# Token rows of a two-stage MLP kernel: stored two tiles at a time, fetched whole, and laid out through DRAM

## The chip, the cores and the metric

The kernel runs on one core of one Trainium2 chip. The metric is the time on the device in microseconds (us); lower is better. A core has a matrix engine (TensorE, PE here, with its weight loads as PEld), VectorE (DVE), ScalarE (ACT), GpSimd (POOL), SyncE (SP), and 16 DMA engines that move data between DRAM and the on-chip memory. SP only issues DMAs in this kernel; POOL issues the indirect ones, whose rows an index picks.

## The reference

Three steps follow one another. All inputs are fp32.

```python
# 1 retention attention: 8 batches x 8 heads, 576 x 64 each, no softmax
scores = (q @ k.T) / 8
ret = scores * where(rel >= 0, gamma[h] ** rel, 0)
x = (ret @ v)                      # as rows: [4608 tokens, 512]
# 2 top-1 mixture of 8 experts, 512 -> 1024 -> 512
idx = argmax(x @ w_gate); gate_w = softmax(x @ w_gate)[idx]
x = gate_w * (maximum(x @ w1[idx], 0) @ w2[idx])
# 3 MLP 512 -> 2048 -> 512
r = maximum(x @ w_in, 0); out = (r * r) @ w_out
```

## The kernel before, in words

Matrix products are made from two or three passes: an fp32 number is split into a high and a low part, and high times high, high times low and low times high are added. The last stage also saves products by a Strassen-like scheme. The program is written out by hand in the order in which it stands on each engine (`manual_schedule`), so each engine runs its instructions in the order of the code.

**Attention** handles 36 tiles of 128 tokens, one per pass of a loop over t. SP loads the tile of four passes ahead (`load(t + 4)`, L364, `in<-att`, up to 1 MB). PE makes the scores (L387), DVE masks them (r, L393), PE makes the output (L435, L439) and the running state (L411), DVE scales it (x, L447) and turns 32 x 32 blocks of it (xr, L449, in one of three buffers). A tile's `put` runs in the next pass: four DMAs of 64 KB (L456, `x_d<-xr`) that write the tile's rows to x_d in DRAM, with the columns of a row permuted in blocks of 32. Small matmuls (lg) give the gate's logits, which go to l_d in DRAM. From these, each token gets a place at its expert: an expert has CT = 5 tiles of 128 places, of which `gidx` names the token to fetch and `sidx` the row to write. The first two tiles of expert 0 are fetched early (lead, L270).

**Experts** run as 64 units, u = 8e + f: expert e and one eighth f of its 1024 hidden columns. A unit is `first` (L806 to L808: 24 matmuls of 320 columns, the hidden values), then ACT and DVE split these (hh L812, hl L813), then `second` (L830 to L832: 15 matmuls of 512 columns, accumulated over the eight units). Units 0 to 5 do a part of the work ahead and are shorter. Beside a unit stand:

- SP loads the weights of seven units ahead (raw, L107) into one of two buffers; ACT and DVE split them one unit later (L113, L115). Side jobs prepare the last stage's weights: SP loads craw (L129), DVE and ACT split it, SP stores it in ws_d (L183, L211).
- POOL fetches the next expert's rows into xs, the only buffer of its kind: for tile i at f = i one `gather`, that is a `tick` (L1050, a 1x1 addition that reads this unit's hidden values and so waits for them) and four indirect DMAs (L270), one for each quarter of a row, since the quarters have to land in four groups of 32 partitions. At f = 5 it fetches five tiles of logits (glg), at f = 7 `finish` scatters the expert's five result tiles to y_d (L291).
- `transp(e+1, i)` at f = i + 2 turns 32 x 32 blocks of xs (DVE, L778) and splits the result into high and low (ACT L782, DVE L783): the columns that the next expert's `first` reads. Because of the permuted columns in x_d, that DVE transpose is all it takes. Expert 0's tiles are fetched whole and turned on PE.

The indices of the quarters, qidx = 4 gidx + a, are made once by `spread`: four matmuls with a table `sel` (256 KB, loaded at L651) and one DVE operation (L788, L789).

**The last stage** reads y_d, and its PE work runs without a pause to the end of the program.

Of the kernel before, what the change touches and what calls it, by code (L numbers as in the profile page):

```python
# [20 lines left out]
NE = 8  # L21
CAP = 640
CT = CAP // 128
NS = NE * CT
# [3 lines left out]
LEAD = 2  # L28
MORE = 6
TINY = 2.0 ** -15 * 1.125  # L30
GROUPS = [(0, 8), (8, 16), (16, 24), (24, 30), (30, 36)]
# [18 lines left out]
def body(ctx, tc, att, tab_v, tab_x, masks, wg, ident, pick, cst, wu, wd, out):  # L50
# [21 lines left out]
    x_d = dram.tile([NTOK, 512], F32, name="x_d")  # L72
    l_d = dram.tile([NTOK, NE], F32, name="l_d")
    y_d = dram.tile([NTOK, 512], F32, name="y_d")
# [4 lines left out]
    sel = places.tile([128, 4, 128], F32, name="sel")  # L79
    ones = places.tile([128, 128], BF16, name="ones")  # L80
# [11 lines left out]
    over = places.tile([1, 1], I32, name="over")  # L92
    gidf = places.tile([128, NS], F32, name="gidf")
    qidx = places.tile([128, 4, NS], I32, name="qidx")

# [160 lines left out]

    def indices(rt, n, inv, gi, si, gf=None):
# [4 lines left out]
        for o in (gi, gf):  # L262
            if o is not None:
                vec.tensor_scalar(out=o, in0=f, scalar1=-1.0, scalar2=0.0, op0=ALU.add, op1=ALU.max)
        g = rt.tile([128, n], F32, tag="g", name="g")
        vec.tensor_scalar(out=g, in0=inv[:, 0:n], scalar1=0.0, scalar2=FAR, op0=ALU.is_equal, op1=ALU.mult)
        vec.scalar_tensor_tensor(out=si, in0=f, scalar=-1.0, in1=g, op0=ALU.add, op1=ALU.add)

    def fetch_rows(xs, src, index):
        pool.indirect_dma_start(  # L270
            out=xs, out_offset=None, in_=src, in_offset=bass.IndirectOffsetOnAxis(ap=index, axis=0),
        )

    def fetch_logits(sm, index, n):
        lg = sm.tile([128, n, NE], F32, tag="lg", name="glg")
        for i in range(n):
            fetch_rows(lg[:, i], l_d[:, :], index[:, i:i + 1])
        return lg


    x_q = x_d.rearrange("n (a c) -> (n a) c", a=4)

# [44 lines left out]
    rt_ps = scope(chain, "rt_ps", 1, PSUM, side="right")  # L327
    with ExitStack() as es:
        tabs = scope(es, "tabs", 1)
# [4 lines left out]
        xr_p = scope(es, "xr_p", 3)  # L334
        sc_ps = scope(es, "sc_ps", 3, PSUM)
# [10 lines left out]

        in_t, vs_t, r_t, st_acc, xp_t = {}, {}, {}, {}, {}
        lead_s = []
# [71 lines left out]
        def out_x(t):  # L420
# [215 lines left out]
        for t in range(NT):  # L636
# [60 lines left out]
    def columns():  # L697
        return [xt_p.tile([128, 4, CAP], F32R, tag=f"xt{s}", name=f"xt{s}") for s in range(2)]
# [52 lines left out]
    with ExitStack() as es:  # L751
# [3 lines left out]
        acc_a = scope(es, "acc_a", 1, PSUM, reuse="tile")  # L755
        xs_t, xt_t, lg_t, h_t, acc, gate = {}, {}, {}, {}, {}, {}

        def gather(e, tiles):
            if e not in xs_t:
                xt_t[e] = columns()  # L760
                xs_t[e] = xs_p.tile([128, CT, 4, 128], F32, tag="xs", name="xs")
            for i in tiles:
                j = CT * e + i
                if e == 0:
                    fetch_rows(xs_t[e][:, i].rearrange("p q c -> p (q c)"), x_d[:, :], gidx[:, j:j + 1])
                    continue
                for q in range(4):
                    fetch_rows(xs_t[e][:, i, q], x_q, qidx[:, q, j:j + 1])

        def transp(e, i):  # L770
# [12 lines left out]
            return lambda: vec.tensor_tensor(out=lo, in0=src, in1=hi.bitcast(F32), op=ALU.subtract)  # L783

        def spread():
            ps = l1_ps.tile([128, 4, NS], F32, tag="l1", name="qi")
            for q in range(4):
                pe.matmul(ps[:, q], sel[:, q], gidf, start=True, stop=True)  # L788
            vec.tensor_scalar(  # L789
                out=qidx, in0=ps, scalar1=4.0, scalar2=cf[:, C_A:C_A + 1], op0=ALU.mult, op1=ALU.add  # L790
            )

# [157 lines left out]
        steps[4]()  # L950
        indices(rt, NS, inv, gidx, sidx, gidf)
        gather(0, range(LEAD, CT))
# [19 lines left out]
        y_p = scope(es, "y_p", 5, reuse="tile")  # L972
        sm = scope(es, "sm", 2, reuse="tile")
        lp = scope(es, "lp", 1, reuse="tile")
        pools["stg"] = scope(early, "stg", 2, side="right", reuse="tile")
# [30 lines left out]
        second(5, tiles)  # L1006
        lg_t[0] = fetch_logits(sm, gidx[:, 0:CT], CT)
        first(0, (1,))
        spread()

        for u in range(NU):
# [32 lines left out]
            if v >= NU + 2:  # L1044
                stream(w_d, v - NU - 2)
            if e + 1 < NE:
                if f <= CT:
                    tick = sm.tile([1, 1], F32, tag="tick", name="tick")
                    here = h_t[u][0][0:1, 0:1].bitcast(F32)
                    pool.tensor_tensor(out=tick, in0=here, in1=here, op=ALU.add)  # L1050
# [4 lines left out]
            if e + 1 < NE:  # L1055
                turns = {3: [0], 4: [1], 5: [2], 6: [3, 4]} if e == 0 else {i + 2: [i] for i in range(CT)}
                rests += [transp(e + 1, i) for i in turns.get(f, [])]
            for f_ in rests[:1]:
# [426 lines left out]
```

## Time and profile before

| what | us |
|---|---|
| median of three runs | 1406.72 |
| the three runs | 1402.28, 1406.72, 1415.77 |
| profiled execution, its time | 1416.54 |
| profiled execution, its span | 1414.7 |

The profiled execution has 1.8 us outside its span, and is the longest of the four. The span divides into attention (to about 198 us, with expert 0's first steps at its end), the experts (to about 640 us), and the last stage. The rows are shown further down; shares of busy time over the whole span average over these three.

### The profile page before, as it was taken

To read this page: it belongs to the slowest core of one execution; us is meant where nothing else is said; L and a number is where in the kernel's file an instruction comes from. 1 tells how busy PE (TensorE), PEld (TensorE's weight loads), DVE (VectorE), ACT (ScalarE), POOL (GpSimd) and SP (SyncE) were. 2 spreads that over 40 slices of the span, in tenths; PEclk is the share of its full clock that TensorE was granted. 3 is DMA by queue.
4 is the path that set the end of the run, shared out by engine and by line. 5 is a ranking of instruction groups with operands and counts; after the bars stand their busy time and mean duration, and the time that the engine had idled before them with its cause. 6 is when DMAs were issued, how large, how long until landed. Compare 5 with 4: busy or idle time off the path is not lost.

```text
span 1414.7 us, 21636 instructions
## 1 busy us (share of the span) xinstructions
PE 1359.7 (96%) x8121; PEld 1161.9 (82%) x8121; DVE 831.8 (59%) x1512; ACT 547.0 (39%) x1064; POOL 375.4 (27%) x408
## 2 busy tenths in 40 slices
PE   8988898999989999899999999999999999999998
PEld 6877787888878889798988888888888888888887
DVE  5666765686967768673785466245742556334422
ACT  1222233453434445342554444244432444234321
POOL 2223345747456474611231013000210003000000
PEclk9999999999999999999999999999999999999999
DMA  9999844666666675656776666567666666665563
GB/s 318 291 287 290 249 137 153 219 217 210 210 197 193 199 246 186 208 173 251 275 272 224 212 233 225 205 208 229 222 234 212 214 207 230 212 234 183 204 212 115
DMA packets 107713, 311.03 MB, mean 220 GB/s; under 512 B 20430, under 2 KB 55758, under 8 KB 85584
## 3 DMA queue, kind: packets, MB, share of 16 engines
q1 hardware_dynamic: 97728, 288.41, 59.9%
q0 software_dynamic: 9872, 21.15, 5.1%
q8 instruction: 66, 1.08, 0.3%
q14 instruction: 47, 0.39, 0.1%
HBM read 257.98 MB, written 52.58 MB: 220 GB/s over the span
## 4 chain that ended last, share of the span: by engine, by line
PE 77%; DMA 10%; issue 6%; POOL 2%; DVE 2%; ACT 1%; another core or an unknown queue 1%; SPq 1%; POOLq 0%; DVEq 0%; ACTq 0%
PE b L1149 23%; PE fa L1223 9%; PE fa L1221 9%; PE fa L1222 9%; DMA in<-att 5%; PE l L808 4%; PE acc L830 4%; PE l L807 4%; PE l L806 4%; PE acc L831 4%; PE acc L832 4%; DMA raw<-wu 1%; POOL xs L270 1%; DMA x_d<-xr 1%
## 5 line engine op out<-in xcount | busy, mean ns | idle before, releaser
L1149 PE MATMUL b<-xt,wq 128*128 128x512 f32 (+1 forms) x1296 | 264.7, 362 | 1.8 <-ACT xt L743 0.7
L1149 PEld LDWEIGHTS b<-xt,wq 128*128 128x128 f32 x1296 | 220.9, 188 | 40.6 <-ACT xt L743 1.1
L1221 PE MATMUL fa<-wq,ch 128*128 128x512 f32 x576 | 224.3, 389 | 0.0
L1223 PE MATMUL fa<-wq,cl 128*128 128x512 f32 x576 | 224.3, 389 | 0.0
L1222 PE MATMUL fa<-wq,ch 128*128 128x512 f32 x576 | 224.3, 389 | 0.0
L1211 DVE TENSOR_TENSOR cl<-g,ch 128x512 fp32r<-128x512 f32 (+1 forms) x160 | 108.9, 689 | 173.7 <-ACT ch L1210 171.2
L734 POOL TENSOR_TENSOR xsum<-yf 128x256 f32<-128x256 f32 x80 | 64.1, 809 | 452.3 <-DVE yf L722 386.9
L270 POOL DMA_INDIRECT xs<-x_d,qidx x140 | 154.9, 1106 | 40.0 <-issue 34.9
L1210 ACT ACTIVATE ch<-g 128x512 fp32r<-128x512 f32 (+1 forms) x160 | 91.5, 584 | 182.4 <-PE fa L1222 181.4
L806 PE MATMUL l<-xt,w 128*128 128x320 f32 (+1 forms) x480 | 150.5, 314 | 6.7 <-issue 5.0
L808 PE MATMUL l<-xt,w 128*128 128x320 f32 (+1 forms) x480 | 150.6, 314 | 5.1 <-issue 5.0
L807 PE MATMUL l<-xt,w 128*128 128x320 f32 (+1 forms) x480 | 150.7, 314 | 4.3 <-issue 4.2
L831 PE MATMUL acc<-w,hh 128*128 128x512 f32 x320 | 128.5, 402 | 3.0 <-issue 3.0
L830 PE MATMUL acc<-w,hh 128*128 128x512 f32 x320 | 129.1, 403 | 2.2 <-issue 1.8
L832 PE MATMUL acc<-w,hl 128*128 128x512 f32 x320 | 127.9, 400 | 2.4 <-issue 2.4
L1223 PEld LDWEIGHTS fa<-wq,cl 128*128 128x128 f32 x576 | 108.1, 188 | 22.5 <-DVE cl L1211 0.2
L1222 PEld LDWEIGHTS fa<-wq,ch 128*128 128x128 f32 x576 | 108.2, 188 | 22.5
L1221 PEld LDWEIGHTS fa<-wq,ch 128*128 128x128 f32 x576 | 108.1, 188 | 22.3
L812 ACT ACTIVATE hh<-l 128x320 fp32r<-128x320 f32 (+2 forms) x128 | 54.6, 436 | 178.4 <-PE l L808 107.3
L1135 ACT ACTIVATE s<-b 128x512 f32<-128x512 f32 (+1 forms) x120 | 66.5, 555 | 104.8 <-PE b L1149 104.6
L813 DVE SCALAR_TENSOR_TENSOR hl<-l,hh 128x320 fp32r<-128x320 f32 (+2 forms) x128 | 59.3, 485 | 79.7 <-ACT hh L812 54.0
L806 PEld LDWEIGHTS l<-xt,w 128*128 128x128 f32 x480 | 90.9, 189 | 9.5 <-issue 4.8
(182 smaller groups left out, 2113.0 us busy)
## 6 DMA issues: line engine op xcount, KB each, us to landing
wq<-ws_d SPq DMA_DIRECT2D x142, 1024.0 KB
raw<-wu SPq DMA_DIRECT2D x62, 512.0 KB
in<-att SPq DMA_DIRECT2D x28, 1024.0 KB
craw<-wd SPq DMA_DIRECT2D x32, 512.0 KB
ws_d<-cw SPq DMA_DIRECT2D x24, 512.0 KB
x_d<-xr SPq DMA_DIRECT2D x144, 64.0 KB
out<-fo SPq DMA_DIRECT2D x32, 256.0 KB
yq<-y_d SPq DMA_DIRECT2D x112, 64.0 KB
```

Of the source, the lines that this page charges most:

```text
L270: pool.indirect_dma_start(out=xs, out_offset=None, in_=src, in_offset=bass.IndirectOffsetOnAxis(ap=index, axis=0),)
L806: pe.matmul(ps, w[:, 0, k], hi[:, k, cs], start=(k == 0), stop=False)
L807: pe.matmul(ps, w[:, 0, k], lo[:, k, cs], start=False, stop=False)
L808: pe.matmul(ps, w[:, 1, k], hi[:, k, cs], start=False, stop=(k == 3))
L830: pe.matmul(acc[i], hh[:, cs], w[:, 0], start=(f == 0), stop=False)
L831: pe.matmul(acc[i], hh[:, cs], w[:, 1], start=False, stop=False)
L832: pe.matmul(acc[i], hl[:, cs], w[:, 0], start=False, stop=(f == 7))
L1149: pe.matmul(ps, w[:, a, c], xc[T][i, b][c], start=(i in (5, 1, 4) and m == 0), stop=(m == 5), skip_group_check=True,)
L1211: vec.tensor_tensor(out=lo[:, o], in0=s, in1=hi[:, o].bitcast(F32), op=ALU.subtract)
L1221: pe.matmul(acc[i], hi[:, cs], w[:, 0], start=(f == 0), stop=False)
L1222: pe.matmul(acc[i], hi[:, cs], w[:, 1], start=False, stop=False)
L1223: pe.matmul(acc[i], lo[:, cs], w[:, 0], start=False, stop=(f == 15))
```

## The change

1. **Store.** The turned tile buffer holds two tiles (still three buffers, now 12 KB in a partition altogether instead of 6). `put` exists only for odd tiles, and stores both with four DMAs of 128 KB. There are 72 such DMAs instead of 144, with the same bytes and the same 512-byte pieces.
2. **Fetch.** For experts 1 to 7 one indirect DMA per tile fetches 128 whole rows into `row` (two buffers). SP then stores them in DRAM (`drop`, r_d, 256 KB), and four more SP DMAs (`lay`, 64 KB each) bring the four quarters back into the four partition groups of xs. `sel`, `spread`, `gidf` and `qidx` are gone.
3. **Order.** With d the unit counted from the start of the expert ahead (d = f of expert n - 1), the steps of tile i stand at the d of four tables. The `tick` is gone. Logits come one tile at a unit, d = 1 to 5. Expert 1's first two tiles are fetched before unit 0, dropped in unit 0, and its turns stand at u = 2 to 6 (before 3, 4, 5, 6, 6).

```diff
+GATHER, DROP, LAY, TURN = (-3, -2, -1, 1, 2), (-1, 0, 1, 3, 4), (0, 1, 2, 4, 5), (2, 3, 4, 5, 6)
...
-            xr = xr_p.tile([128, 4, 4, 32], F32, tag="xr", name="xr")
+            if t % 2 == 0:
+                xr_t[t // 2] = xr_p.tile([128, 8, 4, 32], F32, tag="xr", name="xr")
+            xr = xr_t[t // 2]
             vec.transpose(
-                out=xr.rearrange("q t k j -> q k t j"), in_=x.rearrange("q k (t i) -> q k t i", i=32)
+                out=xr[:, 4 * (t % 2):4 * (t % 2) + 4].rearrange("q t k j -> q k t j"),
+                in_=x.rearrange("q k (t i) -> q k t i", i=32),
             )
+            if t % 2 == 0:
+                return
...
-                rows = x_d[128 * t:128 * t + 128, :].rearrange("(t i) (a c) -> a i t c", i=32, a=4)
+                rows = x_d[128 * t - 128:128 * t + 128, :].rearrange("(t i) (a c) -> a i t c", i=32, a=4)
...
-            if t == 6:
-                sp.dma_start(out=sel, in_=pick)
...
-                for q in range(4):
-                    fetch_rows(xs_t[e][:, i, q], x_q, qidx[:, q, j:j + 1])
+                whole[e, i] = row_p.tile([128, 512], F32, tag="row", name="row")
+                fetch_rows(whole[e, i], x_d[:, :], gidx[:, j:j + 1])
...
+        def drop(e, i):
+            row = whole.pop((e, i))
+            sp.dma_start(out=r_d[CT * e + i - CT], in_=row)
+
+        def lay(e, i):
+            rows = r_d[CT * e + i - CT].rearrange("(t j) (a c) -> a j t c", j=32, a=4)
+            for a in range(4):
+                sp.dma_start(out=xs_t[e][32 * a:32 * a + 32, i], in_=rows[a])
...
         lg_t[0] = fetch_logits(sm, gidx[:, 0:CT], CT)
+        gather(1, range(2))
         first(0, (1,))
-        spread()
...
-            if e + 1 < NE:
-                if f <= CT:
-                    tick = sm.tile([1, 1], F32, tag="tick", name="tick")
...
-                if f < CT:
-                    gather(e + 1, [f])
-                if f == CT:
-                    lg_t[e + 1] = fetch_logits(sm, gidx[:, CT * (e + 1):CT * (e + 2)], CT)
...
+            for n, d in ((e + 1, f), (e + 2, f - 8)):
+                if n >= NE:
+                    continue
+                if n == 1 and d == 0:
+                    drop(1, 0)
+                    drop(1, 1)
+                    gather(1, [2])
+                if n == 1 and d == 1:
+                    drop(1, 2)
...
+                for i in range(CT):
+                    if d == LAY[i]:
+                        lay(n, i)
+                    if d == DROP[i] and (n, i) in whole:
+                        drop(n, i)
+                    if d == GATHER[i]:
+                        gather(n, [i])
+                if 1 <= d <= CT:
+                    logit(n, d - 1)
+                if d in TURN:
+                    rests.append(transp(n, TURN.index(d)))
```

Three places show how the instructions now stand. The first is SP in the middle of attention; before, a load and a tile's four stores take turns:

```order
L364 DMA in<-att 128x2048
L456 DMA x_d<-xr 32x4x128 x4
L107 DMA raw<-wu 128x1024
L364 DMA in<-att 128x2048
L456 DMA x_d<-xr 32x4x128 x4
```

The same place on SP after the change (line numbers are those of the changed kernel, where the store is L457):

```order
L457 DMA x_d<-xr 32x8x128 x4
L106 DMA raw<-wu 128x1024
L360 DMA in<-att 128x2048 x2
L457 DMA x_d<-xr 32x8x128 x4
L360 DMA in<-att 128x2048
```

Two loads now follow one another, and then four stores of twice the size. The second place is POOL across one expert, before the change: the scatters, then five groups of tick and four fetches (the third to fifth are left out), then the logits.

```order
L291 DMA y_d<-y,sidx 4608x512 x5
L1050 TENSOR_TENSOR tick<-hh 1x1
L270 DMA xs<-x_d,qidx 128x128 x4
L1050 TENSOR_TENSOR tick<-hh 1x1
L270 DMA xs<-x_d,qidx 128x128 x4
...
L1050 TENSOR_TENSOR tick<-hh 1x1
L270 DMA glg<-l_d,gidx 128x8 x5
```

POOL across one expert after the change (the fetch line is L267, the scatter L287):

```order
L267 DMA row<-x_d,gidx 128x512 x3
L287 DMA y_d<-y,sidx 4608x512 x5
L267 DMA row<-x_d,gidx 128x512
L267 DMA glg<-l_d,gidx 128x8
L267 DMA row<-x_d,gidx 128x512
L267 DMA glg<-l_d,gidx 128x8 x4
```

An expert's 30 indirect DMAs have become 15, and three row fetches now stand ahead of the scatters. The third place is SP beside the experts, before the change: weight loads, side-job loads and their stores.

```order
L107 DMA raw<-wu 128x1024
L129 DMA craw<-wd 128x1024
L183 DMA ws_d<-cw 128x1024
L107 DMA raw<-wu 128x1024 x2
L183 DMA ws_d<-cw 128x1024
L107 DMA raw<-wu 128x1024
L211 DMA ws_d<-cw 128x512
L211 DMA ws_d<-cw 128x1536
```

SP at such a place after the change (L778 is `drop`, L783 is `lay`, L106 the weight load, L128 craw):

```order
L783 DMA xs<-r_d 32x4x128 x4
L106 DMA raw<-wu 128x1024
L210 DMA ws_d<-cw 128x512
L210 DMA ws_d<-cw 128x1536
L778 DMA r_d<-row 128x512
L106 DMA raw<-wu 128x1024
L128 DMA craw<-wd 128x1024
L783 DMA xs<-r_d 32x4x128 x4
L778 DMA r_d<-row 128x512
```

In five of an expert's eight units SP now has a drop, and in five the four DMAs of a lay, behind the weight load of that unit and ahead of that of the next.

## Rows read from the trace of the kernel before

**Rows 1.** The page, part 1: busy time of each engine over the whole span.

```profile
PE 1359.7 (96%) x8121; PEld 1161.9 (82%) x8121; DVE 831.8 (59%) x1512; ACT 547.0 (39%) x1064; POOL 375.4 (27%) x408
```

**Rows 2.** Windows by stage (experts 1 to 6 in one): busy us by engine, granted clock, DMA share, GB/s.

```profile
core 0: us, PE busy (x) PEld busy (x) DVE busy (x) ACT busy (x) POOL busy (x), PEclk, DMA share, GB/s
40.00:160.50 120.50, 103.67 (x1548) 88.58 (x1545) 81.02 (x169) 27.71 (x68) 33.12 (x28) 0.99 0.93 292
...
227.95:251.03 23.08, 18.15 (x79) 14.46 (x78) 13.08 (x27) 8.33 (x16) 7.66 (x10) 0.85 0.37 124
...
251.03:617.43 366.40, 347.81 (x1874) 309.17 (x1872) 277.17 (x487) 164.80 (x283) 205.99 (x218) 0.98 0.63 209
...
720.00:1414.70 694.70, 690.00 (x3045) 571.21 (x3043) 335.68 (x569) 273.93 (x535) 62.51 (x78) 1.00 0.62 212
```

**Rows 3.** Timeline of SP, first and last of 26 attention loads: start us, us.

```profile
40.69 0.45 SPq L364 DMA_DIRECT2D in<-att  x1
...
160.53 0.40 SPq L364 DMA_DIRECT2D in<-att  x1
```

**Rows 4.** The chain of waits, two tiles of attention and one table load: start us, us.

```profile
41.18 7.72 DMA sel<-pick
...
123.23 1.09 PE sc L387 x16
...
127.07 1.09 PE sc L387 x16
```

**Rows 5.** Waits of engines, attention: us in total, times, longest us.

```profile
DVE xr L449 <- DMA x_d<-xr: 27.9, 22, 2.8
...
PE sc L387 <- DMA in<-att: 21.1, 20, 2.1
...
SPq L456 <- DMA in<-att: 40.5, 26, 2.6
```

**Rows 6.** Window of the busiest 20 us of attention, columns as in rows 2.

```profile
40.00:60.00 20.00, 18.79 (x279) 15.95 (x276) 12.86 (x25) 4.90 (x13) 4.17 (x4) 1.00 0.99 332
```

**Rows 7.** Timeline of PE: first matmul of two units of expert 6 in a row.

```profile
603.55 0.30 PE L806 MATMUL l<-xt,w 128*128 128x320 f32 x1
...
610.49 0.31 PE L806 MATMUL l<-xt,w 128*128 128x320 f32 x1
```

**Rows 8.** Timeline of PE inside the disturbed unit of expert 5.

```profile
518.52 0.40 PE L807 MATMUL l<-xt,w 128*128 128x320 f32 x1
519.95 0.40 PE L808 MATMUL l<-xt,w 128*128 128x320 f32 x1 [1.03 <-issue]
521.38 0.40 PE L806 MATMUL l<-xt,w 128*128 128x320 f32 x1 [1.03 <-issue]
```

**Rows 9.** Timeline of POOL, the fetches beside it.

```profile
493.32 1.21 POOL L291 DMA_INDIRECT y_d<-y,sidx  x1 [15.77 <-ACT y L841]
...
517.44 0.97 POOL L270 DMA_INDIRECT xs<-x_d,qidx  x1
518.72 1.56 POOL L270 DMA_INDIRECT xs<-x_d,qidx  x1 [0.31 <-issue]
...
534.95 0.94 POOL L270 DMA_INDIRECT glg<-l_d,gidx  x1 [0.30 <-issue]
```

**Rows 10.** Groups of instructions by line: busy us, mean ns of one, idle before.

```profile
L270 POOL DMA_INDIRECT xs<-x_d,qidx x140 | 154.9, 1106 | 40.0 <-issue 34.9 <-DVE qidx L789 1.7 <-DVE cv L153 0.5
...
L270 POOL DMA_INDIRECT xs<-x_d,gidx x3 | 2.9, 965 | 19.5 <-DVE g L266 18.9 <-issue 0.6
...
L788 PE MATMUL qi<-gidf,sel 128*128 128x40 f32 x8 | 1.0, 271 | 0.0
```

**Rows 11.** The chain of waits, transfers of 256 KB and less: start us, us.

```profile
219.16 3.94 DMA xs<-x_d,qidx
...
617.17 7.63 DMA y_d<-y,sidx
...
663.64 2.41 DMA yi<-y_d
```

More of the change, by code (lines that the diff above doesn't have):

```diff
@@ L73, in body @@
     l_d = dram.tile([NTOK, NE], F32, name="l_d")
+    r_d = dram.tile([NS - CT, 128, 512], F32, name="r_d")
     y_d = dram.tile([NTOK, 512], F32, name="y_d")
@@ L78, in body @@
     ub = places.tile([128, 128], BF16, name="ub")
-    sel = places.tile([128, 4, 128], F32, name="sel")
     ones = places.tile([128, 128], BF16, name="ones")
@@ L92, in body @@
     over = places.tile([1, 1], I32, name="over")
-    gidf = places.tile([128, NS], F32, name="gidf")
-    qidx = places.tile([128, 4, NS], I32, name="qidx")
     i128 = cf[:, C_I128:C_I128 + 128]
@@ L255, in route, with indices @@
         return first, second, third
-    def indices(rt, n, inv, gi, si, gf=None):
+    def indices(rt, n, inv, gi, si):
         f = rt.tile([128, n], F32, tag="f", name="f")
@@ L261, in indices @@
         )
-        for o in (gi, gf):
-            if o is not None:
-                vec.tensor_scalar(out=o, in0=f, scalar1=-1.0, scalar2=0.0, op0=ALU.add, op1=ALU.max)
+        vec.tensor_scalar(out=gi, in0=f, scalar1=-1.0, scalar2=0.0, op0=ALU.add, op1=ALU.max)
         g = rt.tile([128, n], F32, tag="g", name="g")
@@ L278, in fetch_logits @@
         return lg
-    x_q = x_d.rearrange("n (a c) -> (n a) c", a=4)
     def turn_rows(ps, row):
@@ L328, in body @@
     with ExitStack() as es:
+        xr_p = scope(es, "xr_p", 3)
         tabs = scope(es, "tabs", 1)
@@ L333, in body @@
         r_p = scope(es, "r_p", 2)
-        xr_p = scope(es, "xr_p", 3)
         sc_ps = scope(es, "sc_ps", 3, PSUM)
@@ L345, in body @@
         sts = [tabs.tile([128, 4, 128], F32, name=f"sts{i}") for i in range(4)]
-        in_t, vs_t, r_t, st_acc, xp_t = {}, {}, {}, {}, {}
+        in_t, vs_t, r_t, st_acc, xp_t, xr_t = {}, {}, {}, {}, {}, {}
         lead_s = []
@@ L755, in body @@
         acc_a = scope(es, "acc_a", 1, PSUM, reuse="tile")
-        xs_t, xt_t, lg_t, h_t, acc, gate = {}, {}, {}, {}, {}, {}
+        xs_t, xt_t, lg_t, h_t, acc, gate, whole = {}, {}, {}, {}, {}, {}, {}
         def gather(e, tiles):
-            if e not in xs_t:
-                xt_t[e] = columns()
-                xs_t[e] = xs_p.tile([128, CT, 4, 128], F32, tag="xs", name="xs")
             for i in tiles:
@@ L766, in gather, with places_for, logit @@
                     continue
-                for q in range(4):
-                    fetch_rows(xs_t[e][:, i, q], x_q, qidx[:, q, j:j + 1])
+                whole[e, i] = row_p.tile([128, 512], F32, tag="row", name="row")
+                fetch_rows(whole[e, i], x_d[:, :], gidx[:, j:j + 1])
+        def places_for(e):
+            xt_t[e] = columns()
+            xs_t[e] = xs_p.tile([128, CT, 4, 128], F32, tag="xs", name="xs")
+        def logit(e, i):
+            j = CT * e + i
+            if i == 0:
+                lg_t[e] = sm.tile([128, CT, NE], F32, tag="lg", name="glg")
+            fetch_rows(lg_t[e][:, i], l_d[:, :], gidx[:, j:j + 1])
+        def drop(e, i):
[5 more added lines that the diff above has]
+                sp.dma_start(out=xs_t[e][32 * a:32 * a + 32, i], in_=rows[a])
         def transp(e, i):
@@ L783, in transp @@
             return lambda: vec.tensor_tensor(out=lo, in0=src, in1=hi.bitcast(F32), op=ALU.subtract)
[L785 to L791, printed above, removed]
         def first(u, parts=(0, 1), wait=False):
@@ L950, in body @@
         steps[4]()
-        indices(rt, NS, inv, gidx, sidx, gidf)
+        indices(rt, NS, inv, gidx, sidx)
+        places_for(0)
         gather(0, range(LEAD, CT))
@@ L973, in body @@
         sm = scope(es, "sm", 2, reuse="tile")
+        row_p = scope(es, "row_p", 2, reuse="tile")
         lp = scope(es, "lp", 1, reuse="tile")
@@ L1045, in body @@
                 stream(w_d, v - NU - 2)
-            if e + 1 < NE:
-                if f <= CT:
-                    tick = sm.tile([1, 1], F32, tag="tick", name="tick")
-                    here = h_t[u][0][0:1, 0:1].bitcast(F32)
-                    pool.tensor_tensor(out=tick, in0=here, in1=here, op=ALU.add)
-                if f < CT:
-                    gather(e + 1, [f])
-                if f == CT:
-                    lg_t[e + 1] = fetch_logits(sm, gidx[:, CT * (e + 1):CT * (e + 2)], CT)
-            if e + 1 < NE:
-                turns = {3: [0], 4: [1], 5: [2], 6: [3, 4]} if e == 0 else {i + 2: [i] for i in range(CT)}
-                rests += [transp(e + 1, i) for i in turns.get(f, [])]
+            for n, d in ((e + 1, f), (e + 2, f - 8)):
[7 more added lines that the diff above has]
+                    drop(1, 2)
+                if d == 0:
+                    places_for(n)
+                for i in range(CT):
[9 more added lines that the diff above has]
+                    rests.append(transp(n, TURN.index(d)))
             for f_ in rests[:1]:
```

## The prediction, made before the changed kernel ran

> **What bounds the kernel now.** I read the busy shares first, then windows by stage, then the order of events inside the stages that the change touches. PE is busy for 96% of the span and POOL for 27% [rows 1], so what is gained must be time in which PE stands or runs slowly. The windows tell where that is [rows 2]. From 720 us on PE is busy for 690.0 of 694.7 us: nothing to gain there, and the change touches nothing there. Two stretches are left.
>
> The first is attention. The loop issues 25 more loads between the first and the last one shown, 119.84 us apart [rows 3]: 4.79 us for a tile. Where nothing else held it, the chain has the scores of two following tiles 3.84 us apart, all PE work [rows 4]. So about 0.95 us of each tile is a wait, and the DMA share of 0.93 [rows 2] says for what. The waits agree: DVE waits to overwrite xr until its stores are done (27.9 us in 22 waits), PE waits for loads (21.1 us), and SP itself stands at the stores for 40.5 us until an earlier load ends [rows 5].
>
> The second is the experts. An undisturbed unit takes 6.94 us: the first matmuls of two following units stand at 603.55 and 610.49 [rows 7]. Six experts of eight units should take 6 x 8 x 6.94 = 333.1 us; they take 366.4 [rows 2], 33.3 more. The last two units of the first expert took 23.08 us [rows 2] instead of 13.88, 9.2 more. Together 42.5 us are lost. Looked at closely, the loss is not spread: with all unit starts read as in [rows 7], each of the experts 0 to 6 has one unit of 9 to 15 us, inside which PE starts single matmuls of 0.40 us some 1.43 us apart, "issue" being all that the trace names as a reason [rows 8]; the granted clock falls after that, and so has a mean of 0.85 in the first expert's stretch [rows 2]. These fits fall in late units of an expert. There POOL has been issuing indirect DMAs almost without a break since the scatters: 30 of them from 493.32 to about 536 us, and the fit at 518.5 stands in the middle. POOL's own issues are lengthened beside it too, one of them to 1.56 us, while a whole-row one takes 0.965 in the mean [rows 9, 10]. The last stage, beside which nothing is fetched by index, shows no such fit at a DMA share of 0.62 [rows 2], about that of the experts (0.63). What a fit is, the trace doesn't tell. That POOL's train of fetches brings it on is an inference from place and company, and the forecast hangs on it.
>
> **The change part by part.** The sum starts from the profiled execution, 1416.54 us. It is 9.8 us above the median of the three runs. I take this for a difference in fits, the only part of the trace that looks like chance.
>
> *Stores of two tiles.* They have as many bytes and as many pieces of 512 bytes as before, so what the DMA engines have to do stays. What goes is half of the issues: 72 of 144, and with them places in the queue of SP, at which it stood 40.5 us [rows 5]. DVE may fill the other half of xr while nothing holds it. Upper bound: all of the wait goes, 25 x (4.79 - 3.84) = 24 us. Lower bound: a pair of stores comes in a lump, loads queue behind it, and the first fetches of rows wait for one more tile, a loss of 4.8 us. Between these I go by the DMA engines: at the best share that attention shows, 0.99 [rows 6], 120.5 us at 0.93 would be 120.5 x 0.93 / 0.99 = 113.2, a gain of **7.3 us**. The table load that goes with `sel` is in that (7.72 us in the chain [rows 4], but at 332 GB/s [rows 6] 256 KB are 0.8 us of the engines).
>
> *Spread and sel.* Eight PE records of 0.27 us in all 1.0 us [rows 10] overlap their neighbours; one DVE operation of the same kind. Under 1 us, once: nothing. POOL no longer waits for qidx before expert 1's first fetch.
>
> *Fetches.* 140 indirect DMAs of 1.106 us become 35 of about 0.965, which a whole-row fetch took [rows 10]: 154.9 us of POOL become 34. POOL is not on the path, so this alone is worth nothing. It is worth something only by way of the fits. An expert's 30 indirect DMAs become 15, and the row fetches wait for buffers, so that they fall into two or three short groups. Bounds: 0 (fits have another cause) and 42.5 us (none is left). I take 35: the beginning of each train, some 15 DMAs, runs without a fit in the trace, but the first expert stays crowded.
>
> *Drops and lays.* 35 drops and 140 lays of 64 KB come to SP, behind which stand weight loads, side-job loads and their stores. An expert moved 209 GB/s x 61.07 us = 12.8 MB [rows 2]; a write and a read of 5 x 256 KB more are 2.6 MB, so the DMA share should go from 0.63 to about 0.76, still below the 0.93 of attention. In price: a lay is issued one unit (6.94 us) or more after its drop, and the turn one unit after the lay. Transfers of this size took 2.41 to 3.94 us in the chain, one behind four others 7.63 [rows 11]. So a leg fits into its unit in the usual case: 0 on the path. If the cover is gone, DVE stands in front of the turn and with it PE. The crowded place is the first expert, where units are about 4.2 us and PE must not stand for the turn at u = 2: bounds 0 to 6 us, once; I take **2**.
>
> [...]
>
> *Sum:* 1416.5 - 7.3 - 35 + 2 = **1376 us**.
>
> **The rivals.** *A, as above: the fits mostly go.* For it: the company of the train and the clean stages without one. Own range 1358 (all fits gone, 15 us from attention) to 1393 (25 us of fits gone, 1 or 2 from attention, 4 lost in the first units).
>
> *A', half of the fits stay.* The scatters still stand back to back with the logits beside them. 1416.5 - 7.3 - 21 + 2 = 1390 us.
>
> *B, the fits stay: the change does not do for PE what it does for POOL.* For it: there is no event in the trace that joins PE to POOL, the waits say "issue" alone; and some experts' trains lose under 5 us. Then only the stores count: from the median run, 1406.7 - 7.3 + 2 = 1401 us. [...]
>
> *D, slower: SP's order becomes the bound.* SP issues in order; a drop waits for its row's fetch. The fourth tile's fetch is issued behind five scatters (5 x 1.5 us with the gap, [rows 9]) and lands after up to 7.63 us [rows 11], about 15 us after the expert's end, and its drop stands two units (13.9 us) after the fetch's place. Once SP stands there, the weights, craw, ws_d's stores and the next lay stand behind it; DVE waits for raw at L115 or for xs in front of the turn, hl comes late, PE stands. It decides from the point at which the way from fetch to xs takes more than the two or three units between their places. If one tile of each expert is one unit late, that is 7 x 6.94 = 49 us: 1376 + 49 = **1425 us**. Against it: one leg has a unit to itself, and weights are split five or six units before PE reads them.
>
> **How the numbers follow.** A 0.52, A' 0.13, B 0.22, D 0.13. The prediction is A's, 1376 us. Two runs of this kernel differ by about 1%, so "same" is within 1% of 1406.72: 1392.7 to 1420.8. A lies below it, A' for a good half, B only where attention gives its upper half: 0.62 faster. The rest of A' and B and a mild D make 0.26, the rest of D 0.12 slower. The range goes from A's lower end, 1358, to 1405, which takes in A' and B and leaves out D and the ends of B, some 0.2.
>
> **What would show it.** In the profile after: loads of attention about 4.5 us apart and xr's wait for x_d halved or gone (stores); the units from expert 1 to 6 at 6.94 us each, their sum close to 333 us, and PE's clock at 1.00 there (fits); no wait of DVE's turn or weight split for a DMA over 2 us (drops and lays); SP idle at drops for less than a unit. The prediction is wrong if fits stand beside the short groups too, or if SP's wait at a drop moves the weight loads back until DVE stands.

## The result, and the profile after

The changed kernel takes 1361.44 us (median of five runs, 1358.78 to 1368.36), the kernel before 1406.72: a ratio of 0.9683, 95% interval 0.9638 to 0.9728. The profiled execution of the changed kernel took 1361.44 us with a span of 1359.7, against 1416.54 and 1414.7 before, so 55.0 us of span are to be placed. The profiled execution before stood 9.8 us above its kernel's median: by the medians the gain is 45.3 us, and some 10 of the 55.0 belong to that one execution. One single execution of all those below, of the kernel without ticks on the chip called C, took 1657.63 us at a mean granted clock of 0.753 and is left out of that kernel's ratio.

The first view is part 1 of the page of the changed kernel, the busy times.

```profile
PE 1340.3 (99%) x8113; PEld 1154.0 (85%) x8113; DVE 832.9 (61%) x1510; ACT 546.8 (40%) x1064; POOL 257.8 (19%) x261
```

Against [rows 1] POOL lost 118 us of work, which nobody waited for, and PE 19 us of busy time, most of it in experts 1 to 6 (347.81 to 333.12). The windows by stage of the changed kernel (columns as in [rows 2]: busy us by engine, granted clock, DMA share, GB/s) place the gain. They are attention, expert 0, experts 1 to 6, and the last stage.

```profile
40.00:143.00 103.00, 101.28 (x1532) 87.96 (x1532) 85.04 (x172) 26.63 (x66) 34.64 (x30) 1.00 1.01 343
177.68:228.36 50.68, 46.52 (x229) 41.56 (x228) 30.46 (x50) 20.31 (x34) 16.80 (x15) 0.93 0.73 221
228.36:561.48 333.12, 333.12 (x1873) 303.89 (x1872) 273.50 (x482) 164.09 (x282) 102.44 (x89) 1.00 0.83 273
...
664.00:1359.70 695.70, 690.92 (x3049) 571.74 (x3047) 335.06 (x570) 274.41 (x537) 62.90 (x79) 1.00 0.62 212
```

- **Attention.** Expert 0's units begin at 177.68 us; before, at 198.35: 20.7 us. PE is now busy for 101.28 of 103 us, before for 103.67 of 120.50 [rows 2].
- **Experts 1 to 6** take 333.12 us, 48 units of 6.94 us without exception; before, 366.40 [rows 2]: 33.3 us.
- **Expert 0** takes 50.68 us; before, from 198.35 to 251.03, 52.68: 2.0 us.
- **From there to the end** 798.2 us against 797.3: 0.9 us more. The other kernels below take 796.8 to 798.5 us there, so it does not stand out from what executions differ by.

The sum is 20.7 + 33.3 + 2.0 - 0.9 = 55.1 us. The first matmul of expert 0's units, before and then after (start us, us):

```profile
198.35 0.34 PE L806 MATMUL l<-xt,w 128*128 128x384 f32 x1
```

```profile
177.68 0.34 PE L813 MATMUL l<-xt,w 128*128 128x384 f32 x1
```

In attention the waits of the changed kernel that answer to [rows 5] are these (us in total, times, longest us), the first PE's, the other two SP's own:

```profile
PE sc L383 <- DMA in<-att: 3.4, 3, 2.1
```

```profile
SPq L360 <- PE stp L407: 27.9, 12, 3.8
...
SPq L457 <- DMA in<-att: 0.5, 2, 0.3
```

PE's wait for loads fell from 21.1 to 3.4 us, SP's stand at the stores from 40.5 to 0.5, and DVE's wait for a free xr (27.9) is no longer in the list. SP now stands at the loads, until PE is done with an earlier tile: PE is the bound.

Expert 0 is the place where time was given back. The chain of waits of the changed kernel there (start us, us), and then the waits of DVE and ACT:

```profile
187.43 5.21 DMA xs<-r_d
...
193.22 5.46 DMA raw<-wu
...
204.07 4.73 DMA xs<-r_d
```

```profile
ACT w L112 <- DMA raw<-wu: 12.4, 4, 7.0
DVE xf L793 <- DMA xs<-r_d: 8.7, 2, 5.2
```

The first matmuls of PE at both ends of the two long units, from PE's timeline (start us, us):

```profile
192.42 0.33 PE L813 MATMUL l<-xt,w 128*128 128x384 f32 x1
...
199.91 0.52 PE L813 MATMUL l<-xt,w 128*128 128x384 f32 x1
...
210.29 0.28 PE L813 MATMUL l<-lead,w 128*128 128x256 f32 x1
...
221.42 0.30 PE L813 MATMUL l<-xt,w 128*128 128x320 f32 x1
```

Unit 3 lasted 7.49 us instead of 4.19, unit 4 4.78 instead of 4.19, unit 6 11.13 instead of 6.94: 8.1 us. DVE stood in front of the turns that stand at u = 2 and u = 5, and ACT in front of a weight split (timelines of DVE and ACT):

```profile
192.66 0.71 DVE L793 STREAM_TRANSPOSE xf<-xs 128x512 f32<-128x512 f32 x1 [5.23 <-DMA xs<-r_d]
...
208.92 0.71 DVE L793 STREAM_TRANSPOSE xf<-xs 128x512 f32<-128x512 f32 x1 [3.50 <-DMA xs<-r_d]
```

```profile
193.80 1.06 ACT L112 ACTIVATE w<-raw 128x1024 fp32r<-128x1024 f32 x1 [6.95 <-DMA raw<-wu]
```

In unit 3 both were late, and the weight load was the later one, by 1.1 us. In unit 6 it was the turn: its lay had been issued one short unit before it (202.75 us) and took about 5 us; behind the turn and other work of DVE stands hl, for which PE waits 2.34 us one unit later. Expert 0's granted clock was 0.93 in the mean, so a part of the 8.1 us is likely to be slow matmuls: in a second execution of the same kernel, further down, it was 1.00, and 6.2 us were lost (units of 7.48, 4.19 and 9.85 us).

The opposite is in unit 0, which fell from 7.27 to 6.37 us. Before, the matmuls of `spread` stood in it (PE's timeline of the kernel before):

```profile
200.39 0.34 PE L808 MATMUL l<-xt,w 128*128 128x384 f32 x1
200.56 0.98 PE L788 MATMUL qi<-gidf,sel 128*128 128x40 f32 x8
201.37 0.42 PE L806 MATMUL l<-xt,w 128*128 128x384 f32 x1
```

They put 0.98 us between two matmuls that elsewhere in the unit start 0.17 us apart.

### The profile page after: what moved, and what is told of

Read it like the earlier page. It is cut to its first block, busy times and chain, and to the rows that moved or that the text cites. A ratio compares the mean times of both kernels' runs of the same rounds, so it can differ in the third digit from the quotient of the medians.

```text
span 1359.7 us, 21532 instructions
## 1 busy us (share of the span) xinstructions
PE 1340.3 (99%) x8113; PEld 1154.0 (85%) x8113; DVE 832.9 (61%) x1510; ACT 546.8 (40%) x1064; POOL 257.8 (19%) x261
## 4 chain that ended last, share of the span: by engine, by line
PE 85%; issue 6%; DMA 5%; DVE 2%; SPq 1%; ACT 1%; POOL 1%; POOLq 0%; DVEq 0%; ACTq 0%
PE b L1168 24%; PE fa L1241 10%; PE fa L1240 10%; PE fa L1242 10%; PE l L813 4%; PE l L814 4%; PE l L815 4%; PE acc L837 4%; PE acc L838 4%; PE acc L839 4%; PE x L435 2%; PE sc L383 2%; PE x L431 2%; PE stp L407 1%; DMA idn<-ident 1%
## 5 line engine op out<-in xcount | busy, mean ns | idle before, releaser
L837 PE MATMUL acc<-w,hh 128*128 128x512 f32 x320 | 126.3, 395 | 1.3 <-ACT hh L819 1.1
L838 PE MATMUL acc<-w,hh 128*128 128x512 f32 x320 | 125.8, 393 | 0.0
L1189 DVE TENSOR_TENSOR s<-s,s 128x512 f32<-128x512 f32 (+1 forms) x40 | 25.5, 638 | 113.6 <-ACT s L1154 113.6
L813 PEld LDWEIGHTS l<-xt,w 128*128 128x128 f32 x480 | 90.7, 189 | 5.0 <-DVE hl L820 2.5
L814 PEld LDWEIGHTS l<-xt,w 128*128 128x128 f32 x480 | 90.8, 189 | 2.5 <-DVE xt L798 0.2
```

What stands on the lines that cost most here:

```text
L813: pe.matmul(ps, w[:, 0, k], hi[:, k, cs], start=(k == 0), stop=False)
L814: pe.matmul(ps, w[:, 0, k], lo[:, k, cs], start=False, stop=False)
L837: pe.matmul(acc[i], hh[:, cs], w[:, 0], start=(f == 0), stop=False)
L838: pe.matmul(acc[i], hh[:, cs], w[:, 1], start=False, stop=False)
```

## The experiments

The runs below were on three chips, and the kernel before does not take the same time on them: 1404.89 us on the one called A here, 1372.74 on B, 1372.31 on C (medians of 7, 19 and 23 runs). The first result (1406.72) is of A's kind. Each chip was used at one time only, so chip and time are not told apart. Kernels are compared with the kernel before on their own chip.

**Part 1 alone, on B.** The diff against the kernel before is the part of the change in attention:

```diff
-            xr = xr_p.tile([128, 4, 4, 32], F32, tag="xr", name="xr")
+            if t % 2 == 0:
+                xr_t[t // 2] = xr_p.tile([128, 8, 4, 32], F32, tag="xr", name="xr")
...
+            if t % 2 == 0:
+                return
...
-                rows = x_d[128 * t:128 * t + 128, :].rearrange("(t i) (a c) -> a i t c", i=32, a=4)
+                rows = x_d[128 * t - 128:128 * t + 128, :].rearrange("(t i) (a c) -> a i t c", i=32, a=4)
```

> The kernel before with the stores of two tiles alone (part 1 of the change); fetches, tick, sel and spread stay as before. Theory (the two parts add up, and the fits belong to the fetches): attention ends some 20 us earlier, as in the changed kernel (its expert units began at 177.68 instead of 198.35 us), and the experts 1 to 6 still take 355 to 370 us instead of 333: a median of about 1386 us, 18 to 22 below before. Rival (the fits come from how attention or the stores stand, for instance a queue still full): experts 1 to 6 take about 333 us here too, and the median is about 1365 us.

Measured: 1353.88 us, ratio 0.9865 (0.9846 to 0.9885), 18.9 us less. The window of experts 1 to 6 of this kernel:

```profile
221.11:554.23 333.12, 333.12 (x1873) 303.89 (x1872) 276.92 (x487) 165.31 (x283) 211.27 (x218) 1.00 0.69 230
```

There is no fit, although POOL's trains of 30 fetches are all there (211.27 us of POOL). But the kernel before seems to have no such loss to give on this chip either: its time is 32 us lower than on A. So this run settles the stores (19 us) and nothing about fits.

**Without ticks, and with one fetch for four, on B.** The diffs against the kernel before:

```diff
-                if f <= CT:
-                    tick = sm.tile([1, 1], F32, tag="tick", name="tick")
-                    here = h_t[u][0][0:1, 0:1].bitcast(F32)
-                    pool.tensor_tensor(out=tick, in0=here, in1=here, op=ALU.add)
```

```diff
-                for q in range(4):
-                    fetch_rows(xs_t[e][:, i, q], x_q, qidx[:, q, j:j + 1])
+                fetch_rows(xs_t[e][:, i].rearrange("p q c -> p (q c)"), x_d[:, :], gidx[:, j:j + 1])
```

> The kernel before without the 42 ticks on POOL; the fetches follow one another without waiting for a unit's hidden values. Output unchanged. Theory (fits come with a long unbroken train of indirect DMAs, whatever stands between them): the train of 30 is still there and even closer, so fits stay, 30 to 45 us are lost over the experts, and the median is within 8 us of before. Rival (the tick, a POOL addition that reads what ACT has just written and that PE reads too, makes the fits): experts 1 to 6 take about 333 us and the median falls by about 33 us to some 1373 us.

> The kernel before with one whole-row fetch in place of four quarter fetches for each tile of experts 1 to 7, straight into xs, so the rows stand in the wrong partitions and the output is not the reference's; ticks, scatters, logits in one burst of five, sel and spread stay, no drop and no lay is added. 15 instead of 30 indirect DMAs per expert. Theory (number of fetches in the train): no fits, experts 1 to 6 take 333 to 336 us, attention as before, median about 1370 us. Rival (the tick or the scatter or the burst of logits makes them, or the experts' loss has another cause that the change removed by its order): 355 to 370 us and a median of about 1400 us.

Measured: 1370.55 us (0.9982, 0.9965 to 1.0) and 1371.8 us (0.999, 0.9976 to 1.0004). Both have their experts 1 to 6 in 333.12 us; the windows, first without ticks, then with one fetch:

```profile
239.46:572.58 333.12, 333.12 (x1874) 303.89 (x1872) 277.02 (x487) 165.29 (x283) 195.12 (x182) 1.00 0.69 229
```

```profile
239.90:573.02 333.12, 333.12 (x1874) 303.89 (x1873) 275.02 (x486) 164.72 (x282) 106.49 (x127) 1.00 0.68 229
```

POOL's work halves from 195 to 106 us without a trace in the time: where there are no fits, the number of fetches is worth nothing, as POOL is off the path. For the cause of fits both are inconclusive.

**Fifteen more fetches in the changed kernel, on B.** The diff:

```diff
+                if d == CT:
+                    spare = spare_p.tile([128, 15, 16], F32, tag="spare", name="spare")
+                    for i in range(15):
+                        fetch_rows(spare[:, i], x_d.rearrange("n (a c) -> (n a) c", c=16), gidx[:, i:i + 1])
```

> The changed kernel with 15 more indirect DMAs on POOL for each expert from 1 on, 64 bytes a row into a spare tile that nobody reads, in one piece behind the expert's last logits, so that some 22 indirect DMAs stand in a row and an expert has 30 again. Theory (number of fetches in a train): fits come back, one in most experts, 3 to 8 us each: experts 1 to 6 take 350 to 370 us instead of 333, median 1375 to 1395 us. Rival (not the number, but the bytes or pieces that a quarter fetch moves, or its place beside the tick): no fits, experts 1 to 6 at 333 to 336 us, median within 5 us of the changed kernel's 1361 us.

Measured: 1359.3 us, 0.992 (0.989 to 0.995) of the kernel before there. Experts 1 to 6 take 333.12 us, so no fits, again on a chip that shows none. As the added fetches cost PE nothing there, I take this for the changed kernel on B, which did not run there itself: some 13 us below before, and 5.4 us above the kernel with part 1 alone, which has nothing to pay for in expert 0.

**The changed kernel, and part 1 alone, on A.** The kernels as above.

> The changed kernel as it is, beside the kernel before on the same chip, since the chip of the last runs gave 1372.7 us for the kernel before and showed no fits even with its train of fetches. Theory (fits belong to some chips or hours, and there the change takes them away; elsewhere only the stores count): where before takes about 1373 us, this takes about 1359 us, 13 to 14 less (20 from attention, 6 to 7 given back in the first expert); where before takes about 1406 us, some 1361 us. Rival (the first gain of 45 us was the change's own): a ratio of about 0.968 wherever it runs.

> Once more the kernel before with the stores of two tiles alone. On a chip where before takes about 1373 us: 1354 us, 19 below before and about 5 below the whole change, since the fetches' part only costs there. On a chip where before takes about 1406 us, the two theories part: if fits belong to the train of 30 fetches they stay, 1380 to 1390 us and some 25 above the whole change; if not, about 1355 us.

Measured: 1362.12 us for the whole change (0.968, 0.9609 to 0.9752), 1387.95 us for part 1 alone (0.9841, 0.9765 to 0.9918). Here the two part: the same kernel that took 1353.88 us on B is 25.8 us slower than the whole change, and 16.9 us below before. Windows of experts 1 to 6, the whole change first, then part 1 alone:

```profile
225.59:560.07 334.48, 333.39 (x1873) 303.90 (x1872) 273.89 (x483) 163.50 (x282) 99.82 (x89) 1.00 0.83 272
```

```profile
229.77:593.41 363.64, 347.57 (x1873) 310.94 (x1872) 275.83 (x485) 163.56 (x282) 203.69 (x217) 0.97 0.63 210
```

Part 1 alone loses 30.5 us to fits, one unit of 9.1 to 14.6 us in each of the experts 1 to 6. The whole change has a single unit of 8.29, and that is no fit: PE waits there 1.08 us for DVE's hl (PE's timeline of the whole change).

```profile
533.96 0.42 PE L813 MATMUL l<-xt,w 128*128 128x320 f32 x1 [1.08 <-DVE hl L820]
```

The two kernels with the fetches' part that follow on A have 333.14 and 333.16 us for experts 1 to 6, no fit either. Part 1 alone also shows what parts the chips: its two profiled executions, 1392.04 us here and 1353.79 on B, differ by 38.2 us, and experts 0 to 6 alone (415.65 us against 377.49) by as much. A fit of part 1 alone in PE's timeline, POOL's timeline beside it, and three windows through it:

```profile
312.75 0.31 PE L811 MATMUL l<-xt,w 128*128 128x320 f32 x1 [0.27 <-issue]
314.15 0.31 PE L812 MATMUL l<-xt,w 128*128 128x320 f32 x1 [1.10 <-issue]
...
316.98 0.43 PE L812 MATMUL l<-xt,w 128*128 128x320 f32 x1 [1.78 <-issue]
318.41 0.43 PE L813 MATMUL l<-xt,w 128*128 128x320 f32 x1 [1.00 <-issue]
```

```profile
287.73 1.01 POOL L291 DMA_INDIRECT y_d<-y,sidx  x1 [15.10 <-ACT y L846]
...
291.66 1.60 POOL L291 DMA_INDIRECT y_d<-y,sidx  x1 [0.30 <-issue]
...
315.07 0.95 POOL L270 DMA_INDIRECT xs<-x_d,qidx  x1 [0.30 <-issue]
321.19 0.62 POOL L1055 TENSOR_TENSOR tick<-hh 1x1 f32<-1x1 f32 x1 [5.18 <-ACT hh L817]
```

```profile
310.00:318.00 8.00, 3.70 (x19) 2.99 (x18) 1.83 (x5) 1.14 (x3) 4.93 (x6) 0.81 0.18 49
318.00:321.00 3.00, 2.59 (x9) 2.47 (x9) 2.52 (x3) 2.30 (x5) 0.00 (x0) 0.50 0.24 86
321.00:324.40 3.40, 3.40 (x14) 2.72 (x13) 3.40 (x7) 1.96 (x4) 2.75 (x3) 0.87 0.77 228
```

It begins some 25 us after the train's first scatter, as in the kernel before. But POOL's last fetch was done at 316.0 us, and PE still stood for 0.96 of the 1.78 us before 316.98 and for all of the 1.00 us before 318.41; and the DMA share was 0.18. An issue of 1.60 us stands some 20 us ahead of the fit, so long issues on POOL are not a mark of it, as the prediction took them to be. At its end PE's clock was granted at 0.50 for 3 us, and then 0.87 in the mean. So this fit is not just PE waiting for a POOL issue under way, and not a crowd of transfers. The stores of two tiles don't prevent fits; the fetches' part of the change does.

**Late turns for expert 1, on A.** The diff against the changed kernel:

```diff
-                if d in TURN:
-                    rests.append(transp(n, TURN.index(d)))
+                for i in range(CT):
+                    if d == ((3, 4, 5, 6, 6) if n == 1 else TURN)[i]:
+                        rests.append(transp(n, i))
```

> The changed kernel with the turns of expert 1 at units 3, 4, 5, 6, 6 as before, instead of 2 to 6; nothing else. Theory (in the first expert the way through DRAM is longer than a short unit, and DVE waits 5.2 and 3.5 us in front of two turns): the units of 7.49 and 11.13 us fall to about 4.2 and 7 us, and the median is 5 to 7 us below the changed kernel's. Rival (the weight loads behind the drops are late, and DVE waits for these instead): the wait moves to L114's weight split, 0 to 2 us gained.

Measured: 1357.55 us (0.9652, 0.9584 to 0.9721), 4.6 us below the changed kernel on the same chip; the runs (1356.63 to 1361.09 against 1358.03 to 1366.11) overlap a little. The waits of DVE and ACT in expert 0 of this kernel:

```profile
ACT w L112 <- DMA raw<-wu: 11.7, 4, 8.5
DVE w L114 <- ACT w L112: 10.0, 3, 9.0
```

The wait for xs is gone, and unit 6 takes 6.96 us instead of 9.85 on that chip. Units 3 and 4 get longer, 8.03 and 5.15 us instead of 7.48 and 4.19: what is late next is a weight load, which stands on SP behind two drops and the four DMAs of a lay. Theory and rival each had one of the two units. The windows of expert 0, the changed kernel on A and then this one, give the net gain:

```profile
176.78:225.59 48.81, 43.46 (x229) 38.82 (x228) 30.08 (x50) 20.32 (x34) 16.28 (x14) 1.00 0.71 227
```

```profile
176.14:223.56 47.42, 44.70 (x230) 40.11 (x229) 29.97 (x50) 20.73 (x34) 16.27 (x15) 0.96 0.73 234
```

It is 1.4 us. The rest of the 3.8 us between these two profiled executions lies where the turns of expert 1 don't reach (1.3 us in experts 1 to 6, the unit of 8.29 us; 0.6 ahead of expert 0; 0.4 behind expert 6), so late turns can claim 1.4 us of the 4.6.

**Eight small stores for a pair, on A.** The diff against the changed kernel:

```diff
-                for a in range(4):
-                    sp.dma_start(
-                        out=rows[a], in_=xr[32 * a:32 * a + 32].rearrange("q t k j -> q t (k j)")
-                    )
+                for s in range(2):
+                    for a in range(4):
+                        sp.dma_start(
+                            out=rows[a][:, 4 * s:4 * s + 4],
+                            in_=xr[32 * a:32 * a + 32, 4 * s:4 * s + 4].rearrange("q t k j -> q t (k j)"),
+                        )
```

> The changed kernel with the two tiles of a store sent as eight DMAs of 64 KB instead of four of 128 KB; still after the odd tiles, from the same buffers. Theory (what held attention was the number of DMAs in SP's queue, of which only so many are under way before SP waits): the loss comes back, attention is 12 to 20 us longer, median 10 to 18 us above the changed kernel's. Rival (it was DVE's wait for a free xr, so room for two tiles in a buffer is what counts): within 4 us of the changed kernel.

Measured: 1387.44 us, 25.3 above the changed kernel on that chip. Expert 0 begins at 206.35 us instead of 176.78, so attention got 29.6 us longer, more than expected. That is 8.0 us later than in the kernel before (198.35), which has as many DMAs to a tile in another order; where these 8.0 us come from is open. The window of attention of this kernel, and SP's waits and timeline there:

```profile
40.00:160.50 120.50, 103.59 (x1481) 89.22 (x1479) 84.26 (x166) 25.85 (x64) 33.07 (x27) 0.94 0.87 279
```

```profile
SPq L458 <- DMA in<-att: 45.3, 25, 3.3
```

```profile
58.69 1.83 SPq L360 DMA_DIRECT2D in<-att  x2
60.62 7.97 SPq L458 DMA_DIRECT2D x_d<-xr  x8
```

The bytes, the buffers and the place in the program are the changed kernel's; only the number of DMAs differs, and with it the size of one. The trace shows how that acts: SP spends 7.97 us on eight stores, standing at some of them until a load has ended. In the records of the traces before and after, SP's DMAs in attention carry eight semaphores in turn, and each waits on its own, that is for the DMA eight places before it: all 144 before and all 103 after, from 36 to 165 us. In that order, with two loads and eight stores to a pair, the seventh and eighth store wait for the two loads just issued, and the next load stands behind them in SP's list; the waits of this kernel agree, 45.3 us for loads in 25 times. With two loads and four stores, the DMA eight places back belongs to an earlier pair, and the stores of the changed kernel waited 0.5 us for loads.

**Six buffers for xr, on C.** The diff against the kernel before:

```diff
+        xr_p = scope(es, "xr_p", 6)
         tabs = scope(es, "tabs", 1)
...
-        xr_p = scope(es, "xr_p", 3)
```

> The kernel before with six buffers of one tile for xr instead of three, the same 12 KB in a partition as the changed kernel's; the stores stay 144 DMAs of 64 KB. Theory (the number of DMAs in SP's queue holds attention): within 4 us of before, the wait of DVE for xr is gone but SP still stands some 40 us at the stores. Rival (the free buffer for xr counts): attention 15 to 20 us shorter, as with the stores of two tiles.

Measured: 1372.12 us, ratio 0.9996 (0.9974 to 1.0017). SP's waits in attention of this kernel:

```profile
SPq L456 <- DMA in<-att: 43.9, 27, 2.6
```

DVE's wait for xr has left the list, SP stands as long as before (40.5 us, [rows 5]), and no gain is measured; the interval leaves room for at most 3.6 us. In its profiled execution expert 0 begins at 193.45 us, in those of the two kernels below with three small buffers on C at 198.2, but the medians show nothing of that. The free buffer was not what held attention for 19 us.

**The three tests of fits once more.** The same kernels as above; they ran on C.

> The kernel before without the ticks, once more, for the case that the chip shows fits (before about 1405 us). Theory (length of the train of indirect DMAs): fits stay in the experts 1 to 6, 355 to 370 us there, median within 10 us of before. Rival (the tick makes them): 333 us there, median about 1372 us. Where before takes about 1373 us, the run tells nothing of fits.

> The kernel before with one whole-row fetch in place of four quarter fetches, straight into xs (the rows stand in the wrong partitions, so the output is not the reference's), ticks and the burst of logits kept, once more for a chip with fits. Theory (number of fetches in a train): 15 per expert as in the changed kernel, no fits, experts 1 to 6 at 333 to 337 us, median about 1372 us where before takes 1405. Rival (the tick, or the way through DRAM and SP's new order, and not the number): fits stay, within 10 us of before.

> The changed kernel with 15 more indirect DMAs per expert, 64 bytes a row into a tile that nobody reads, once more for a chip with fits. Theory (number of fetches in a row): fits come back, experts 1 to 6 at 345 to 370 us, median 1372 to 1395 us. Rival (it takes the bytes or the 512-byte pieces of quarter fetches): 333 us there, median about 1361 us.

Measured, in this order: 1374.34 us (1.0014, 0.9993 to 1.0036), 1369.78 us (0.9992, 0.9971 to 1.0013), 1361.61 us (0.9938, 0.9915 to 0.9961). All three have 333.12 us for the experts 1 to 6. C shows no fits: the kernel with six buffers, whose experts are those of before, has 333.12 us there too:

```profile
237.53:570.65 333.12, 333.12 (x1874) 303.95 (x1872) 276.68 (x487) 165.14 (x283) 204.04 (x218) 1.00 0.69 230
```

So the three tell nothing of fits.

## Why the prediction was right, and where it wasn't

The forecast was 1376 us and faster, the measured time is 1361.44, inside the range. Its two large terms had the right sign and were both too small; that the result came from a chip with fits was luck, since the prediction didn't know that its largest term hangs on this. Step by step:

- **Stores of two tiles: right in sign, mis-sized.** The term was 7.3 us; it measured 20.7 in the profile, and alone 18.9 on B and 16.9 on A by the medians. The step that failed is "Between these I go by the DMA engines": it took a DMA share of 0.99 at 332 GB/s for a ceiling. The changed kernel has 1.01 and 343 GB/s over 103 us, and PE is the bound. The same bytes (35 MB in either window) took 0.93 x 120.5 = 112 us of share before and 1.01 x 103.0 = 104 after, so the share has no fixed price and is no measure of work left. At 0.93 there was room for 20.7 us. The upper bound, from the PE-only step of 3.84 us a tile, came within 3.3 us. What held the loop was the number of DMAs in SP's list, as eight small stores and six buffers showed: SP's stand at the stores until loads had ended is 40.5 us before, 43.9 with six buffers and 45.3 with eight small stores, all with five DMAs to a tile, and 0.5 in the changed kernel, with three.
- **Fits: right, and larger.** The term was 35 of 42.5 us. All 33.3 us of experts 1 to 6 went, and the fit in expert 0 too. That part 1 alone keeps 30.5 us of fits on A, while the whole change and its two variants there have none, shows that the fetches' part removes them. That it is the halved train, as the prediction inferred, is not shown: ticks, quarter fetches, the place of the fetches and SP's new work changed with it, and the runs that part these fell on chips without fits. It stays open, and so does what a fit is.
- **The baseline.** The prediction took the 9.8 us between the profiled execution and the median for a difference in fits between runs; that stays not shown, as only the one execution was traced. The runs showed more: the kernel before takes 1404.89 us on A and about 1372.5 on B and C. On B and C the rival "the fits stay" has its mirror image: there are none to take away, and the gain is the stores' less what expert 0 costs, 0.6 to 0.8% as far as the two kernels with idle fetches tell. The changed kernel itself did not run there.
- **Drops and lays: right for experts 1 to 6, too low for expert 0.** 2 us with bounds of 0 to 6 were given; 8.1 us were lost in units 3, 4 and 6, and 6.2 in the second execution. The bound's failing was to look at the turn at u = 2 alone; the fourth tile's lay, issued at 202.75 us, came late for u = 5, and the weight load behind drops and a lay was the last to come in unit 3. A lay took 4.73 and 5.21 us in the chain, longer than the short units of 4.19 us and than the 2.41 to 3.94 us of [rows 11]. By its own sign, no wait of a turn or a weight split for a DMA over 2 us, the prediction was wrong there. In the later experts SP did stand at the lays, but no unit lost anything in this profile (1.4 us in the second execution). The DMA share was 0.83, above the 0.76 estimated: that sum kept the 61.07 us that an expert took with its fits; over 55.5 us it gives 0.83.

```profile
SPq L783 <- DMA r_d<-row: 38.5, 18, 4.9
```

- **Rival D, slower by SP's order,** showed its mechanism, in expert 0 alone, where units last 4.19 us and not 6.94: the way through DRAM (about 5 us for a lay in the chain) is longer than the one and shorter than the other. That is the point at which it was said to decide, only for the lay alone. (The 7.63 us of [rows 11], read there as one transfer behind four others, begin at 617.17, with the second of five scatters.)
- **Rival B** is out on A: something in the fetches' part of the change does act on PE. Experts 1 to 6 take 334.48 us with it and 363.64 with part 1 alone. By what road it acts is not shown: in the fit shown PE stood for 1.00 us while POOL was idle.
- **Spread and sel: put at nothing, worth 0.9 us.** The matmuls did not overlap their neighbours, as the forecast had it, but stood between them, and unit 0 lost the 0.9 us with them: it takes 7.26 to 7.29 us in every kernel here that has `spread`, 6.36 to 6.39 in every one without. That is within the "under 1 us" given.

The errors add up: 13.4 us more from the stores and 7.5 more from fits, 6.1 lost beyond the 2 in expert 0, and 0.9 gained from spread against 0.9 more behind the experts: 14.8 us, the way from the sum's 1376.2 to 1361.4. The range's lower end, by its own terms (all 42.5 us of fits, 15 from attention), is 1359 and not 1358.

## What to carry to other kernels

Where a queue issues many small DMAs beside large loads, count DMAs and not bytes: half as many stores of twice the size gave 17 to 21 us, while more buffers gave nothing. Bound such a gain by the step of the engine that comes next (here PE's 3.84 us a tile), not by the DMA share. And a detour through DRAM was free here only where the unit that covered it was longer than the transfer (a lay of 4.73 to 5.21 us, units of 4.19 and 6.94): check the first, short units on their own, and all that a queue holds back there: later turns for expert 1 freed one unit and left the next to a late weight load, 1.4 us in all by the traces.

## What the runs showed of the hardware that was not expected

- The same kernel takes 1404.89 us on one chip and 1372.74 and 1372.31 on two others. In the kernel with part 1 alone the difference is the fits: single matmuls 0.7 to 2.1 us apart in one unit of each of the experts 1 to 6, some 25 us into a train of indirect DMAs in the two shown, with the clock granted at 0.50 for 3 us at the end of the one windowed here. Where a change to such a kernel is judged, which chip it ran on counted for as much as the change; whether it is the chip or the time is open.
- In such a fit PE stood for 1.00 us with POOL idle, at a DMA share of 0.18, so neither explains it by itself.
- The DMA share went to 1.01 over 103 us, with 343 GB/s, where the kernel before had 0.93 and 292 over 120.5 us for the same bytes.
- SP's DMAs in attention carry eight semaphores in turn, and each waits for the one eight places before it (144 DMAs before, 103 after). With five DMAs to a tile SP stood 40.5 us at the stores until loads had ended, with three 0.5.
